# Late modulation vectors on TensorE instead of VectorE, and FFN loads in program order

## The chip, the core and the metric

The kernel runs on one core of one Trainium2 chip. A core has engines that each run their own queue of instructions in order: TensorE (PE in the profile, with its weight loads as PEld), VectorE (DVE), ScalarE (ACT), GpSimd (POOL) and SyncE (SP), which here only starts transfers. Sixteen DMA engines move the data between the large memory (DRAM) and the core's working memory. The metric is the device time of one execution in microseconds (us), the median of several runs. Before the change it is 1277.53 us.

## The reference, cut to what matters

One transformer layer on 2048 rows of 1024 values. Six modulation vectors of 1024 values come from silu(c) times w_mod (1024 x 6144). The first two, sa and ca, shift and scale the first layer norm; ga gates the attention's output; sb and cb shift and scale the second layer norm; gb gates the FFN's output.

```python
def reference(A_x, A_k_cache, A_v_cache, A_wq, A_wo, B_x, B_w_gate, B_w_up, B_w_down, c, w_mod):
    ...
    x = A_x
    mod = (_silu(c) @ w_mod).reshape(c.shape[0], 6, 1, -1)
    sa, ca, ga, sb, cb, gb = (mod[:, 0].copy(), mod[:, 1].copy(), mod[:, 2].copy(), mod[:, 3].copy(), mod[:, 4].copy(), mod[:, 5].copy())
    h = _layernorm(x, axis=-1) * (1 + ca) + sa
    x = x + ga * _A_ref(h, A_k_cache, A_v_cache, A_wq, A_wo)
    h = _layernorm(x, axis=-1) * (1 + cb) + sb
    x = x + gb * _B_ref(h, B_w_gate, B_w_up, B_w_down)
    return x
```

_A_ref is attention: 32 heads of 128, keys and values of four groups cut to their last 512 rows, softmax, and the output projection wo (4096 x 1024). _B_ref is a gated FFN of width 3584: silu(x w_gate) * (x w_up), then w_down.

## The kernel before, in words

All of it lies in fast_path. (A second function, general_path, stands behind a flag for inputs whose scores could grow too large; with these inputs it isn't entered.)

The 2048 rows are cut into four chunks (cc) of 512, the width of one matmul. A first loop runs over 128 steps k, one for each chunk and head: step k computes the scores of head k (emit_s), the queries of head k + 3 (emit_q), then whatever tasks are due at step k (run_tasks), then the weighted sum over the values of head k - 1 (emit_o). A second pair of loops does the FFN: for each chunk seven groups (fg) of four 128-wide slices of the hidden width (emit_gu), then the down projection in two halves (dh) of four row tiles (emit_down). Task numbers go on counting there, from 129.

Tasks are put down by `at(k, f, ...)`: the projection by wo (load_wo, emit_wo, from step 13 on, eight tasks for each quarter of a chunk's heads), the layer norms (plan_ln: statistics, normalised rows, a transposing transfer, and eight affine steps ln_affine with scale and shift), the transposes of attention outputs (xpose_o), the late modulation vectors, and a bound on the scores that sets the flag.

The first two modulation vectors are needed at once and are computed in the opening by mod_cols on TensorE. The other four are late. spread_c writes silu(c) to DRAM and reads it back to all partitions. load_wmT fetches 128 columns of w_mod with a transposing transfer, so that each partition holds one column; mod_dot multiplies this by silu(c) and sums along the row on VectorE, which gives 128 values of the vector as a column (eight such for one vector). cb and sb are used as columns; cb gets 1 added by add_one. The gates ga and gb are needed as rows on all partitions: store_gate turns the columns on VectorE and writes them to DRAM, load_gate reads them back.

The order of instructions is set by a scheduler that works with its own estimates, except where `pin` keeps an instruction in program order. A switch in `stage` says what pin holds: in the first loop transfers and listed VectorE instructions; in the FFN loops neither, since `stage.update(dma=False, steps=False)` stands between the loops. All loads go through SP's one queue by way of fetch (line 664). An instruction on a queue that waits holds up those behind it.

Buffers: PSUM tiles of 512 values come from a set of four (`mm`), for q_ps, a_ps, o_ps and d_ps; pairs of score or gate-and-up tiles from another. Weights of wq, gate and up use seven blocks of set B, with one more block in the storage of v_sb once attention is over (every second FFN group puts a quarter there); wo, down tiles, oq and oT use twelve blocks of set C; hT, the modulated inputs, and pieces of w_mod use four buffers of hpool.

In the FFN loops before the change, a group's gate and up tiles are loaded (load_gu) in the program just ahead of their use, and the first half's down tiles of chunk 0 after its groups:

```python
            if (cc, fg) != (0, 0):
                load_gu(cc, fg)
            if cc > 0:
                load_wd(cc, 0, fg)
```

The scheduler may move them.

Of the kernel before, what the change touches and what calls it, by code (L numbers as in the profile page):

```python
# [9 lines left out]
ALU = mybir.AluOpType  # L10
AX = mybir.AxisListType
BF16 = mybir.dt.bfloat16
FP32 = mybir.dt.float32
# [575 lines left out]
def fast_path(ctx, tc, flag, A_x, A_k_cache, A_v_cache, A_wq, A_wo, B_x, B_w_gate, B_w_up,  # L589
# [3 lines left out]
    nc = tc.nc  # L593
    P = 128
    _, S, D = A_x.shape
    _, Hkv, Sk, Dh = A_k_cache.shape
# [6 lines left out]
    TCW = 512  # L603
    NTC = S // TCW
    QT = TCW // P
    DT = D // P
# [5 lines left out]
    NFG = FT // 4  # L612
# [11 lines left out]
    wm_v = w_mod.rearrange("(dt p) n -> p dt n", p=P)  # L624
# [4 lines left out]
    const = ctx.enter_context(tc.tile_pool(name="const", bufs=1))  # L629
    xpool = ctx.enter_context(tc.tile_pool(name="xres", bufs=1))  # L630
    hpool = ctx.enter_context(tc.tile_pool(name="hT", bufs=4))
# [3 lines left out]
    wk = ctx.enter_context(tc.tile_pool(name="work", bufs=2))  # L635
    sm = ctx.enter_context(tc.tile_pool(name="small", bufs=4))
    psp = ctx.enter_context(tc.tile_pool(name="psum", bufs=4, space=bass.MemoryType.PSUM))
    dp = ctx.enter_context(tc.tile_pool(name="dram", bufs=4, space=bass.MemoryType.DRAM))
# [7 lines left out]
    def blkC(name, shape, dt=BF16):  # L646
        return pc_.tile(shape, dt, name=name, tag="C")

    def mm(name, shape=(P, 512), dt=FP32):
        return psp.tile(list(shape), dt, name=name, tag="mm", bufs=4)  # L650
# [7 lines left out]
    stage = {"dma": True, "steps": False}  # L658

    def pin(ins, what="steps"):  # L660
        return tc.keep_in_program_order(ins) if stage[what] else ins

    def fetch(out, in_):
        pin(nc.sync.dma_start(out=out, in_=in_), "dma")

    def load(out, in_):
        with nc.allow_non_contiguous_dma(reason="weight slice"):
            fetch(out=out, in_=in_)
# [33 lines left out]
    for kv in range(Hkv):  # L702
        pin(nc.sync.dma_start_transpose(
            out=kT[:, kv, :], in_=A_k_cache[0, kv, k0:k0 + W, :]), "dma")
# [10 lines left out]
    ones_bf = const.tile([P, P], BF16, name="ones_bf")  # L715
# [15 lines left out]
    sa, ca1, sb, cb1 = (modT[:, i, :] for i in range(4))  # L731
    ga_bc = const.tile([P, D], FP32, name="ga_bc")
    gb_bc = const.tile([P, D], FP32, name="gb_bc")
# [7 lines left out]
    sil_r = const.tile([DT, P], BF16, name="sil_r")  # L741
# [3 lines left out]
    siluc = const.tile([P, DT], BF16, name="siluc")  # L745
# [12 lines left out]

    c_d = dp.tile([DT, P], BF16, name="c_d", tag="c_d", bufs=1)
    c_bc = const.tile([P, D], BF16, name="c_bc")
    gcol = [const.tile([P, 32], FP32, name=f"gcol{n}") for n in range(2)]
    grow = const.tile([P, 32], FP32, name="grow")
    for n in range(2):
        nc.gpsimd.memset(gcol[n], 0.0)
    wm_cols = {}
    col_d = {}  # L770

    def spread_c():
        fetch(out=c_d, in_=sil_r)
        fetch(out=c_bc.rearrange("p (a b) -> p a b", a=DT), in_=c_d.partition_broadcast(P))

    def load_wmT(vec, j):
        if j % 4 == 0:
            wm_cols[(vec, j // 4)] = hpool.tile([P, 4, D], BF16, name="wmT", tag="hT")
        c0 = vec * D + j * P
        pin(nc.sync.dma_start_transpose(out=wm_cols[(vec, j // 4)][:, j % 4, :],  # L780
                                        in_=w_mod[:, c0:c0 + P]), "dma")

    def mod_dot(vec, j, dst):
        t = wm_cols[(vec, j // 4)]
        junk = wk.tile([P, D], BF16, name="junk", tag="junk", bufs=1)
        pin(nc.vector.scalar_tensor_tensor(out=junk, in0=t[:, j % 4, :], scalar=1.0, in1=c_bc,
                                           op0=ALU.mult, op1=ALU.mult,
                                           accum_out=dst[:, j:j + 1]))

    def add_one(dst):  # L790
        pin(nc.vector.tensor_scalar(out=dst, in0=dst, scalar1=1.0, scalar2=None, op0=ALU.add))

    def store_gate(n):
        d = dp.tile([DT, P], FP32, name="col_d", tag="col_d", bufs=2)
        pin(nc.vector.transpose(out=grow, in_=gcol[n]))
        for q in range(4):
            fetch(out=d[:, 32 * q:32 * q + 32], in_=grow[32 * q:32 * q + DT, :])
        col_d[n] = d

    def load_gate(n, dst):  # L800
        fetch(out=dst.rearrange("p (a b) -> p a b", a=DT), in_=col_d[n].partition_broadcast(P))

    tasks = {}

    def at(k, f, *a):
        tasks.setdefault(k, []).append((f, a))


    hT = {}
# [112 lines left out]
    for t in range(QT):  # L922
        ln_stats(t)
        n = ln_norm(t, t % 2 == 0)
# [5 lines left out]
    for half in range(DH):  # L930
# [6 lines left out]
        for n in range(4 * LEAD):  # L937
            dt, g = (4 * half + n // LEAD, n % LEAD) if half == 0 else (4 + n % 4, n // 4)
            nc.tensor.matmul(q0_ps[g],  # L939
                             lhsT=wq_tiles[(0, 0, dt // 4)][:, dt % 4, g * P:(g + 1) * P],  # L940
                             rhs=hT[("h1", 0)][:, dt, :], start=(dt == 0), stop=(dt == DT - 1))
# [168 lines left out]
            nc.vector.tensor_tensor(out=x1, in0=f, in1=x1, op=ALU.add)  # L1110


    at(0, spread_c)
    for vec, dst, starts in ((2, gcol[0], (1, 9)), (4, cb1, (17, 25)), (3, sb, (33, 41)),
                             (5, gcol[1], (51, 61))):
        for part in range(2):
            for i in range(4):
                at(starts[part] + 2 * i, load_wmT, vec, 4 * part + i)
                at(starts[part] + 2 * i + 3, mod_dot, vec, 4 * part + i, dst)
        k = starts[1] + 10  # L1120
        if vec == 4:
            at(k, add_one, cb1)
        elif vec in (2, 5):
            at(k, store_gate, vec // 5)
            at(k + 3, load_gate, vec // 5, gb_bc if vec == 5 else ga_bc)
    for tt in range(QT, S // P):
        cc, t = divmod(tt, QT)
        at(max((cc - 1) * H - 16, 0) + 2 + 2 * t, load_x, tt)
# [32 lines left out]
    def load_gu(cc, fg):  # L1161

        for nm, v in (("wg", wg_v), ("wu", wu_v)):
            for i in range(2):
                spare = (cc * NFG + fg) % 2 == 1 and nm == "wu" and i == 1
                t = v_blk if spare else blkB(nm, [P, 4, 512])
                load(t, v[:, 4 * i:4 * i + 4, fg * 512:(fg + 1) * 512])
                gu_w[(cc, fg, nm, i)] = t
# [16 lines left out]
    def load_wd(cc, dh, fg):  # L1185
        t = blkC("wd", [P, 4, 512])
        load(t, wd_v[:, 4 * fg:4 * fg + 4, dh * 512:(dh + 1) * 512])
        wd_tiles[(cc, dh, fg)] = t
# [23 lines left out]
    for k in range(NU + 1):  # L1212
# [9 lines left out]
        run_tasks(k)  # L1222
        if k >= 1:
            emit_o(k - 1)
    stage.update(dma=False, steps=False)
    for cc in range(NTC):
        for fg in range(NFG):
            if (cc, fg) != (0, 0):
                load_gu(cc, fg)
            if cc > 0:  # L1230
                load_wd(cc, 0, fg)
            for fi in range(4):
                emit_gu(cc, 4 * fg + fi)
                run_tasks(NU + 1 + (cc * NFG + fg) * 4 + fi)
        for dh in range(DH):
            if dh > 0 or cc == 0:
                for fg in range(NFG):
                    load_wd(cc, dh, fg)
            for t in range(QT):
                last = cc == NTC - 1 and dh == DH - 1 and t == QT - 1  # L1240
                emit_down(cc, dh, t, (256, 128, 128) if last else (512,))
# [41 lines left out]
```

## Time and profile before

| what | value |
|---|---|
| median of 3 runs | 1277.53 us (1277.34 to 1278.34) |
| the profiled execution | 1277.53 us |
| its span, first to last instruction | 1275.8 us |
| mean granted TensorE clock | 0.998 |
| VectorE dot products (L786) | 32, 38.9 us busy |
| transposing loads of w_mod (L780) | 32, on SP |
| DMA, mean over the span | 160 GB/s |

The profile is one execution. Busy times of different engines overlap, so their sum says nothing; what ends the kernel is read from the chain of waits and from the idle time ahead of each engine's instructions. A matmul's record lasts longer than the time after which the next one starts; the pace is read from starts. PEclk gives the granted clock in tenths, by slices of 32 us.

### The profile page before, as it was taken

How to read it: one execution, taken by the hardware profiler on the slowest of the kernel's cores; microseconds unless marked ns; L12 is line 12 of the kernel's file. 1: busy time of each engine (PE TensorE's matmuls, PEld its weight loads, DVE VectorE, ACT ScalarE, POOL GpSimd, SP SyncE). 2: the span in 40 equal slices, each digit the busy share in tenths (PEclk: the TensorE clock that was granted, in tenths of full speed). 3: DMA queues.
4: the chain of work that ended last, by engine and by line, in shares of the span. 5: the costliest groups of instructions: out<-in, count | busy, mean ns of one | idle time of the engine just before them, and what ended most of it. 6: DMA issues, size and time to landing. Idle time of an engine off the chain costs nothing.

```text
span 1275.8 us, 17958 instructions
## 1 busy us (share of the span) xinstructions
PE 1256.8 (99%) x7396; PEld 641.0 (50%) x7537; DVE 606.8 (48%) x1325; ACT 333.7 (26%) x433; POOL 1.3 (0%) x10
## 2 busy tenths in 40 slices
PE   8999999999999999999999999999999999999998
PEld 4555555555555555555554444444444444444444
DVE  4575578966587755576663641221122112221122
ACT  3543333343343433334341111011100111011100
POOL 0000000000000000000000000000000000000000
PEclk9999999999999999999999999999999999999999
DMA  9998556785646563446467474455436454454301
GB/s 269 223 223 197 156 132 187 169 186 154 164 127 173 141 172 118 141 124 141 127 214 231 152 244 137 136 190 172 158 119 211 134 178 151 141 190 136 128 22 48
DMA packets 307868, 204.46 MB, mean 160 GB/s; under 512 B 145601, under 2 KB 305345, under 8 KB 307778
## 3 DMA queue, kind: packets, MB, share of 16 engines
q1 hardware_dynamic: 302866, 199.03, 54.6%
q10 hardware_dynamic: 4912, 4.20, 1.0%
q8 instruction: 61, 1.00, 0.3%
q14 instruction: 29, 0.24, 0.1%
HBM read 165.94 MB, written 4.21 MB: 133 GB/s over the span
## 4 chain that ended last, share of the span: by engine, by line
PE 97%; DVE 1%; issue 1%; ACT 0%; DMA 0%
PE gu_ps L1177 30%; PE a_ps L1095 17%; PE q_ps L1018 17%; PE d_ps L1197 15%; PE o_ps L1063 9%; PE s_ps L1031 8%; PE q_ps L939 1%; DVE junk L954 0%; DVE st L815 0%; DMA x<-in_A_x_dram 0%; PE mod_ps L753 0%; ACT pT L1033 0%; DVE qT L915 0%; ACT xn L831 0%; PE h_ps L926 0%
## 5 line engine op out<-in xcount | busy, mean ns | idle before, releaser
L1033 ACT ACTIVATE pT<-s_ps 128x1024 bf16<-128x1024 f32 x256 | 248.9, 1020 | 357.9 <-PE s_ps L1031 230.5
L1095 PE MATMUL a_ps<-wo,oT 128*128 128x512 bf16 x987 | 240.0, 379 | 1.9
L1018 PE MATMUL q_ps<-hT,wq 128*128 128x512 bf16 x999 | 236.9, 379 | 0.3 <-DVE modT L755 0.3
L1183 DVE TENSOR_TENSOR guT<-gu_ps,sg 128x512 bf16<-128x512 f32 x112 | 77.4, 691 | 283.1 <-ACT sg L1182 283.1
L1177 PE MATMUL gu_ps<-hT,wg 128*128 128x512 bf16 x875 | 209.7, 379 | 1.1
L1182 ACT ACTIVATE sg<-gu_ps 128x512 bf16<-128x512 f32 x112 | 66.9, 597 | 488.7 <-PE gu_ps L1177 431.7
L1197 PE MATMUL d_ps<-wd,guT 128*128 128x512 bf16 (+2 forms) x934 | 193.2, 366 | 0.9
L915 DVE CAST qT<-q_ps 128x512 bf16<-128x512 f32 x128 | 88.2, 690 | 159.7 <-PE q_ps L1018 157.3
L1177 PE MATMUL gu_ps<-hT,wu 128*128 128x512 bf16 x659 | 162.0, 379 | 0.7
L1095 PEld LDWEIGHTS <-oT 128*128 128x128 bf16 x1024 | 100.2, 98 | 120.6
L1018 PEld LDWEIGHTS <-wq 128*128 128x128 bf16 x1000 | 97.8, 98 | 117.7 <-issue 0.3
L1197 PEld LDWEIGHTS <-guT 128*128 128x128 bf16 x952 | 90.9, 98 | 103.0
L1063 PEld LDWEIGHTS <-pT 128*128 128x128 bf16 x2048 | 126.8, 98 | 31.0 <-issue 0.4
L1177 PEld LDWEIGHTS <-wg 128*128 128x128 bf16 x896 | 87.6, 98 | 105.5
L1063 PE MATMUL o_ps<-v_sb,pT 128*128 128x130 bf16 x2048 | 137.3, 220 | 0.1
L1031 PE MATMUL s_ps<-qT,kT 128*128 128x512 bf16 x467 | 129.3, 379 | 2.9 <-ACT pT L1033 0.6
L1177 PEld LDWEIGHTS <-wu 128*128 128x128 bf16 x672 | 65.8, 98 | 79.3
L1050 DVE TENSOR_TENSOR oq<-o_ps,rl 128x256 bf16<-128x256 f32 (+2 forms) x256 | 100.4, 419 | 3.7 <-issue 0.2
L1201 DVE TENSOR_TENSOR f<-d_ps,gb_bc 128x512 f32<-128x512 f32 (+2 forms) x34 | 22.4, 660 | 147.1 <-PE d_ps L1197 147.1
L1031 PEld LDWEIGHTS <-kT 128*128 128x128 bf16 x512 | 44.9, 98 | 31.5 <-issue 1.3
L1103 DVE TENSOR_TENSOR acc<-a_ps,acc 128x512 f32<-128x512 f32 x64 | 44.1, 688 | 32.8 <-PE a_ps L1095 32.6
L1177 PE MATMUL gu_ps<-hT,v_sb 128*128 128x512 bf16 x220 | 56.9, 379 | 0.2
(76 smaller groups left out, 401.4 us busy)
## 6 DMA issues: line engine op xcount, KB each, us to landing
wq<-in_A_wq_dram SPq DMA_DIRECT2D x64, 512.0 KB
wo<-in_A_wo_dram SPq DMA_DIRECT2D x64, 512.0 KB
wg<-in_B_w_gate_dram SPq DMA_DIRECT2D x56, 512.0 KB
wd<-in_B_w_down_dram SPq DMA_DIRECT2D x56, 512.0 KB
wu<-in_B_w_up_dram SPq DMA_DIRECT2D x42, 512.0 KB
v_sb<-in_B_w_up_dram SPq DMA_DIRECT2D x14, 512.0 KB
x<-in_A_x_dram SPq DMA_DIRECT2D x16, 256.0 KB
wm<-in_w_mod_dram SPq DMA_DIRECT2D x4, 1024.0 KB
```

The lines of the kernel that those rows point to most:

```text
L915: nc.vector.tensor_copy(out=t, in_=q_ps)
L1018: nc.tensor.matmul(q_ps, lhsT=wq_tiles[(cc, h // 4, dt // 4)][:, dt % 4, (h % 4) * P:(h % 4 + 1) * P], rhs=hT[("h1", cc)][:, dt, :], start ...
L1031: nc.tensor.matmul(s_ps[:, i, :], lhsT=kT[:, kv, j * P:(j + 1) * P], rhs=qT[g], start=True, stop=True)
L1033: nc.scalar.activation(out=p[:, 2 * jj:2 * jj + 2, :], in_=s_ps, func=ACT.Exp, scale=scale)
L1050: nc.vector.tensor_tensor(out=dst, in0=ps[:, s0:s0 + cnt, 0:Dh], in1=sc, op=ALU.mult)
L1063: nc.tensor.matmul(o_slot["ps"][:, s_, :], lhsT=pT[g][:, j, t * P:(t + 1) * P], rhs=v_sb[:, kv, j, 0:VN], start=(j == 0), stop=(j == WT - 1))
L1095: nc.tensor.matmul(a_ps, lhsT=oT[(cc, 2 * q + i)][:, hh % 4, t * P:(t + 1) * P], rhs=wo_tiles[(cc, q, dh, i)][:, hh % 4, :], start=(hh == ...
L1103: nc.vector.tensor_tensor(out=acc[(cc, t)][:, dsl], in0=a_ps, in1=acc[(cc, t)][:, dsl], op=ALU.add)
L1177: nc.tensor.matmul(ps[:, n, :], lhsT=gu_w[(cc, fg, nm, dt // 4)][:, dt % 4, fi * P:(fi + 1) * P], rhs=hT[("h2", cc)][:, dt, :], start=(dt ...
L1182: nc.scalar.activation(out=g, in_=ps[:, 0, :], func=ACT.Silu)
L1183: nc.vector.tensor_tensor(out=guT[(cc, fg)][:, fi, :], in0=ps[:, 1, :], in1=g, op=ALU.mult)
L1197: nc.tensor.matmul(d_ps, lhsT=guT[(cc, f // 4)][:, f % 4, t * P:(t + 1) * P], rhs=wd_tiles[(cc, dh, f // 4)][:, f % 4, c0:c0 + w], start=( ...
```

## The change

Two things are changed.

The late vectors: load_rows now fetches w_mod as it lies, four 128-row blocks by one vector's 1024 columns (1 MB) in one transfer. sil32 holds silu(c) repeated over 32 columns; it is made in the opening by eight VectorE multiplications. mod_rows multiplies on TensorE: two vectors at a time, as four strips of 512 values, each to its own 32 PSUM partitions, in two parts of 16 matmuls (steps 5 and 13 for ga and cb, 21 and 29 for gb and sb). VectorE copies the first part out and adds it to the second; the four rows go to DRAM (row_d). load_gate reads a gate back to all partitions, load_cols reads cb or sb back as columns, 1024 single values, and for cb adds 1 on VectorE.

The FFN's transfers: pin still holds transfers in program order in the FFN loops. load_gu is called one group ahead. In chunk 0 the first half's down tiles are loaded two at a time in its last four groups.

```diff
--- before.py
+++ after.py
@@ -758,47 +758,48 @@
-    c_d = dp.tile([DT, P], BF16, name="c_d", tag="c_d", bufs=1)
-    c_bc = const.tile([P, D], BF16, name="c_bc")
-    gcol = [const.tile([P, 32], FP32, name=f"gcol{n}") for n in range(2)]
-    grow = const.tile([P, 32], FP32, name="grow")
-    for n in range(2):
-        nc.gpsimd.memset(gcol[n], 0.0)
-    wm_cols = {}
-    col_d = {}
-    def spread_c():
-        fetch(out=c_d, in_=sil_r)
-        fetch(out=c_bc.rearrange("p (a b) -> p a b", a=DT), in_=c_d.partition_broadcast(P))
-    def load_wmT(vec, j):
-        if j % 4 == 0:
-            wm_cols[(vec, j // 4)] = hpool.tile([P, 4, D], BF16, name="wmT", tag="hT")
-        c0 = vec * D + j * P
-        pin(nc.sync.dma_start_transpose(out=wm_cols[(vec, j // 4)][:, j % 4, :],
-                                        in_=w_mod[:, c0:c0 + P]), "dma")
-    def mod_dot(vec, j, dst):
-        t = wm_cols[(vec, j // 4)]
-        junk = wk.tile([P, D], BF16, name="junk", tag="junk", bufs=1)
-        pin(nc.vector.scalar_tensor_tensor(out=junk, in0=t[:, j % 4, :], scalar=1.0, in1=c_bc,
-                                           op0=ALU.mult, op1=ALU.mult,
-                                           accum_out=dst[:, j:j + 1]))
-    def add_one(dst):
-        pin(nc.vector.tensor_scalar(out=dst, in0=dst, scalar1=1.0, scalar2=None, op0=ALU.add))
-    def store_gate(n):
-        d = dp.tile([DT, P], FP32, name="col_d", tag="col_d", bufs=2)
-        pin(nc.vector.transpose(out=grow, in_=gcol[n]))
-        for q in range(4):
-            fetch(out=d[:, 32 * q:32 * q + 32], in_=grow[32 * q:32 * q + DT, :])
-        col_d[n] = d
-    def load_gate(n, dst):
-        fetch(out=dst.rearrange("p (a b) -> p a b", a=DT), in_=col_d[n].partition_broadcast(P))
+    sil32 = const.tile([P, DT, 32], BF16, name="sil32")
+    for dt in range(DT):
+        nc.vector.tensor_scalar(out=sil32[:, dt, :], in0=ones_bf[:, 0:32],
+                                scalar1=siluc[:, dt:dt + 1], scalar2=None, op0=ALU.mult)
+    wm_rows = []
+    row_part = []
+    row_d = {}
+    def load_rows(vec, part):
+        t = hpool.tile([P, 4, D], BF16, name="wmr", tag="hT")
+        load(t, wm_v[:, 4 * part:4 * part + 4, vec * D:(vec + 1) * D])
+        wm_rows.append(t)
+    def mod_rows(n, part):
+        ps = mm("row_ps")
+        tiles = [wm_rows.pop(0) for _ in range(2)]
+        for k in range(4):
+            for i in range(4):
+                nc.tensor.matmul(ps[32 * i:32 * i + 32, :], lhsT=sil32[:, 4 * part + k, :],
+                                 rhs=tiles[i // 2][:, k, (i % 2) * 512:(i % 2 + 1) * 512],
+                                 start=(k == 0), stop=(k == 3))
+        if part == 0:
+            r = blkC("row", [P, TCW], FP32)
+            nc.vector.tensor_copy(out=r, in_=ps)
+            row_part.append(r)
+        else:
+            r = row_part.pop()
+            nc.vector.tensor_tensor(out=r, in0=ps, in1=r, op=ALU.add)
+            d = dp.tile([4, TCW], FP32, name="row_d", tag="row_d", bufs=2)
+            fetch(out=d, in_=r[0:P:32, :])
+            row_d[n] = d
+    def load_gate(n, k, dst):
+        fetch(out=dst.rearrange("p (a b) -> p a b", a=2),
+                          in_=row_d[n][k:k + 2, :].partition_broadcast(P))
+    def load_cols(n, k, dst, add_one):
+        src = row_d[n][k:k + 2, :].rearrange("a (b p) -> p (a b)", p=P)
+        with nc.allow_non_contiguous_dma(reason="1024 values to columns"):
+            fetch(out=dst, in_=src)
+        if add_one:
+            nc.vector.tensor_scalar(out=dst, in0=dst, scalar1=1.0, scalar2=None, op0=ALU.add)
     tasks = {}
@@ -1110,19 +1111,14 @@
             nc.vector.tensor_tensor(out=x1, in0=f, in1=x1, op=ALU.add)
-    at(0, spread_c)
-    for vec, dst, starts in ((2, gcol[0], (1, 9)), (4, cb1, (17, 25)), (3, sb, (33, 41)),
-                             (5, gcol[1], (51, 61))):
+    for n, vecs in enumerate(((2, 4), (5, 3))):
         for part in range(2):
-            for i in range(4):
-                at(starts[part] + 2 * i, load_wmT, vec, 4 * part + i)
-                at(starts[part] + 2 * i + 3, mod_dot, vec, 4 * part + i, dst)
-        k = starts[1] + 10
-        if vec == 4:
-            at(k, add_one, cb1)
-        elif vec in (2, 5):
-            at(k, store_gate, vec // 5)
-            at(k + 3, load_gate, vec // 5, gb_bc if vec == 5 else ga_bc)
+            k = 16 * n + 8 * part
+            at(k, load_rows, vecs[0], part)
+            at(k + 2, load_rows, vecs[1], part)
+            at(k + 5, mod_rows, n, part)
+        at(16 * n + 15, load_gate, n, 0, gb_bc if n else ga_bc)
+        at(16 * n + 16, load_cols, n, 2, sb if n else cb1, n == 0)
     for tt in range(QT, S // P):
         cc, t = divmod(tt, QT)
         at(max((cc - 1) * H - 16, 0) + 2 + 2 * t, load_x, tt)
@@ -1222,18 +1218,23 @@
         run_tasks(k)
         if k >= 1:
             emit_o(k - 1)
-    stage.update(dma=False, steps=False)
+    stage.update(steps=False)
     for cc in range(NTC):
         for fg in range(NFG):
-            if (cc, fg) != (0, 0):
-                load_gu(cc, fg)
+            n = cc * NFG + fg + 1
+            if n < NTC * NFG:
+                load_gu(*divmod(n, NFG))
             if cc > 0:
                 load_wd(cc, 0, fg)
+            elif fg >= NFG - 4:
+                for i in range(2):
+                    if 2 * (fg - NFG + 4) + i < NFG:
+                        load_wd(0, 0, 2 * (fg - NFG + 4) + i)
             for fi in range(4):
                 emit_gu(cc, 4 * fg + fi)
                 run_tasks(NU + 1 + (cc * NFG + fg) * 4 + fi)
         for dh in range(DH):
-            if dh > 0 or cc == 0:
+            if dh > 0:
                 for fg in range(NFG):
                     load_wd(cc, dh, fg)
             for t in range(QT):
```

## The prediction

> **What bounds the kernel now.** I read the page first (busy shares, slices, chain), then the stretches by window, then TensorE's own waits, then the chain in order of time, and last the timeline where the change puts new work.
>
> ```profile
> span 1275.8 us, 17958 instructions
> PE 1256.8 (99%) x7396; PEld 641.0 (50%) x7537; DVE 606.8 (48%) x1325; ACT 333.7 (26%) x433; POOL 1.3 (0%) x10
> PEclk9999999999999999999999999999999999999999
> PE 97%; DVE 1%; issue 1%; ACT 0%; DMA 0%
> ...
> 0.00:20.00 20.00, 14.59 (x167) 8.31 (x170) 9.71 (x29) 7.40 (x14) 1.34 (x10) 1.00 1.02 320
> 100.00:200.00 100.00, 99.16 (x674) 54.62 (x686) 64.50 (x149) 37.37 (x42) 0.00 (x0) 1.00 0.66 172
> 900.00:1000.00 100.00, 99.53 (x456) 45.30 (x463) 21.44 (x31) 8.96 (x15) 0.00 (x0) 1.00 0.50 169
> ...
> PE warm_ps L727 <- POOL warm_w L721: 1.5, 1, 1.5
> PE s_ps L1031 <- ACT pT L1033: 0.6, 2, 0.3
> ...
> 745.32 10.74 PE gu_ps L1177 x49
> 756.11 10.74 PE gu_ps L1177 x49
> ...
> 22.17 4.24 PE L939 MATMUL q_ps<-hT,wq 128*128 128x512 bf16 x12
> ```
>
> TensorE is 99% busy, but that row alone proves nothing, because one record lasts 379 ns and records overlap. The chain pieces prove it: one piece of the FFN starts 10.79 us after the other (756.11 - 745.32) and holds 50 matmuls (49 recorded, one missing), so one 128x512 matmul takes 10.79 / 50 = 0.2158 us, piece after piece. The program has 1024 such matmuls for q, 512 for scores, 1024 for wo, 1792 for gate and up, 896 for down: 5248, of which 24 fall in the opening. 5224 x 0.2158 = 1127.3 us. A head's 16 narrow o matmuls fill what is left of an early step: 3.49 - 12 x 0.2158 = 0.90 us; 128 heads give 115.5 us. Sum 1242.8; from the end of the opening (26.4 us) this reaches 1269.2, and the last matmuls end near 1270.5. So between the opening and the tail TensorE loses about 1.3 us in all. The longest waits in its list belong to the opening, none to the FFN. Nothing outside the first 26 us and the last 5 us can be won; whatever is added to TensorE's queue is paid in full.
>
> **What the Trainium skill says.** "TensorE: Matmul & The Clock Gate", Part 3, "Measured speedup vs the span model": matmuls with 32 stationary columns, each with its output at another 32-partition strip, run side by side; three in columns gave 2.38x, four in rows 3.07x. "TensorEngine Tiling (Array Packing)", "Key Properties": a change of the tiling mode drains TensorE. No record of before has a tile other than 128 columns wide, so the trace neither agrees nor disagrees. "DMA: Bandwidth & Descriptors", "Rules for kernel authors": a transfer with a strided last dimension becomes one descriptor per element; before has no such transfer of 4-byte pieces. The first page, Part 1, has TensorE at half clock after an idle window of some 3.4 us; here the 12 q matmuls at 22.17 us average 0.353 us against 0.216, which agrees in kind.
>
> **The change, part by part.** All times against the profiled execution: 1277.53 us, 1.7 more than its span, and equal to the median.
>
> (1) Removed, on VectorE: 32 dot products (group L786, 38.9 us at 1216 ns, with 32 accumulator reads of 83 ns), two 32x32 transposes, and the 32 transposing loads and eight small stores on SP. VectorE is 48% busy and TensorE waits for it for less than 2 us in all, in the opening. Gain: nothing on the path. Also gone is SP's stop between writing c_d and reading c_bc.
>
> (2) Added, on TensorE: four bursts of 16 matmuls (L779), at steps 5, 13, 21 and 29, 32 columns wide, 512 elements each. One after the other they cost 64 x 0.2158 = 13.8 us. Successive ones go to different column strips, so I take the 3.07x of the skill for four: 4.5 us (estimate). Each burst enters and leaves the narrow mode; a drain I take as what a record lasts beyond the pace, 0.379 - 0.216 = 0.163 us (estimate); eight make 1.3. Sum 5.8 us. Bounds: perfect fourfold overlap and no drain 3.5 us; no overlap 13.8 + 1.3 = 15.1 us. There is no idle TensorE time to hide any of it.
>
> Do the bursts wait for their data? The first needs two 1 MB loads, which SP can issue from about 25 us. Ahead of the second's end lie some 3.5 MB; at the 210 GB/s of the stretch from 40 to 60 us this is 17 us: landed by 42, used at about 45. The others have 5 to 10 us more. Nothing, with 3 us of margin for the first.
>
> (3) Added, eight small multiplications on VectorE in the opening (sil32, about 0.13 us each as a small VectorE row such as siluc's copy shows): 1.0 us before the third tile's statistics. On TensorE the order also changes: the first two mod_ps groups (64 matmuls) now stand ahead of the third and fourth tiles' transposes. Both end before the last w_mod tile arrives (19.90 us, the DMAs at 320 GB/s), which ends last there. Zero, within -1.7 and +1: the matmuls at half clock are worth 4.24 - 12 x 0.2158 = 1.65 us if the clock should now stay up.
>
> (4) Added, a wait on VectorE. Scale cb1 now comes by way of DRAM: row_d is written, then ga_bc and the 8x128 column values are fetched, and L802 adds one. L802 stands, in VectorE's fixed order, just after xn of the seventh tile and ahead of the acc copy of step 15. In before these are:
>
> ```profile
> 84.14 0.69 DVE L915 CAST qT<-q_ps 128x512 bf16<-128x512 f32 x1 [0.32 <-PE q_ps L1018]
> 84.75 0.54 DVE L834 TENSOR_SCALAR xn<-x,mv 128x1024 bf16<-128x1024 bf16 x1
> 85.87 0.69 DVE L1101 COPY acc<-a_ps 128x512 f32<-128x512 f32 x1 [0.58 <-PE a_ps L1095]
> 89.16 1.89 PE L1095 MATMUL a_ps<-wo,oT 128*128 128x512 bf16 x8
> ...
> 24.83 0.38 SPq L664 DMA_DIRECT2D c_d<-sil_r  x1
> 29.91 0.36 SPq L664 DMA_DIRECT2D c_bc<-c_d  x1
> ```
>
> VectorE reaches L802 at 85.3 + 2.9 (two bursts) = 88.2 us. SP: row_d waits for the second burst's sum. That burst ends at about 73.5 + 2.9 = 76.4, the sum at 77.4. Behind it on SP, by before's durations: row_d 0.3, wo 0.6, wq 0.5, four oT transposes 6.0, hT 1.3, wq 0.5, ga_bc 0.7, the column fetch about 0.8: issued at 88.1. Landing: the only small transfer that before waits for, c_d, took from 25.2 to 29.9 = 4.7 us under a full queue. So 92.8. How long can TensorE go on? The psum pool has four buffers: a_ps of step 15, two of o_ps, q_ps of step 16; the fifth request, a_ps of step 16, comes at 89.16 + 2.9 = 92.1. After landing VectorE still has L802, one half of statistics (0.68) and the acc copy (0.69) before a buffer is free: 92.8 + 0.16 + 1.37 + 0.1 = 94.4. TensorE waits 94.4 - 92.1 = 2.3 us; with a little for the 1024 pieces, 2.6 us. Bounds: 0 (landing within 2.3 us) and about 6 (landing after 8). The second set, step 32, is read only by the later affines: nothing.
>
> (5) The FFN's loads. Now every one stays in program order, and a group's four gate and up loads are issued one group ahead. They need buffers that group fg-1 gave back, so each starts at the start of group fg and is needed 13.8 us later (64 x 0.2158). Demand: five loads of 0.52 MB in 13.8 us = 190 GB/s, in the last four groups of the first chunk six, 228 GB/s; the opening ran at 320. Before has loads behind other loads on the same queue and no TensorE wait, so there is nothing to gain; what can be lost is a load stuck behind one whose buffer is not free. The candidates are the last two down tiles of a half (issued some 5 us before the half ends, as the two of before at 1241.07, needed 4.3 us after it starts) with the next chunk's second group behind them, which has 24 + 14 us left; and SP's read of flag, which stands ahead of the third group's loads and is over before group 0 (20.7 us with the wo matmuls) is. Zero.
>
> Sum: 5.8 + 2.6 = 8.4 us: 1277.5 + 8.4 = 1285.9.
>
> **The rivals.** About 0.2%, 2.6 us, can be told from no change.
> - The VectorE wait doesn't reach TensorE (landing in 2 us): 1277.5 + 5.8 = 1283.3. For it: the queue is lighter without transposing loads (stretch 80 to 100 us: DMA share 0.80). Against: SP is late by the row_d wait. 17%.
> - The narrow matmuls don't overlap: 15.1 + 2.6 = 17.7, 1295.2. For it: nothing in the trace shows overlap, and their weights are loaded anew for each. Against: the skill's measurement. 16%.
> - Program order makes FFN loads late, say 3 us in each of the four groups with six loads: 8.4 + 12, 1298. Against: the margins of (5). 5%.
> - Not slower: fourfold overlap without drains (3.5), no VectorE wait, and the opening's q matmuls at full clock (-1.65), because transposes and warm-up matmuls now run nearer to them: +1.9, 1279.4. It decides from 1280.1 down. Against: the idle time before 19.90 us, which lets the clock fall, is set by the loads and stays. 12%.
>
> **How the numbers follow.** The forecast 50% (own range 1282.5 to 1290), the others as given. 1280.5 to 1296 takes in the first three and leaves out the last two. Slower: 50 + 17 + 16 + 5 = 88; of the last 12, 2 faster (the opening gains more) and 10 within.
>
> **What would show it.** Burst records 128*32 spaced by about 70 ns rather than 216; a TensorE wait of 2 to 3 us near 92 us, put down to VectorE or the column fetch; L802's idle time of 4 to 5 us; FFN windows at 99.5 busy again; 26.4 us as the opening's end. Wrong if the chain shows DMA inside the FFN, or if the FFN ends earlier relative to its start than now.

## The result, and the profile after

The changed kernel takes 1283.48 us, the median of 6 runs (1283.05 to 1285.36), against 1277.19 us for the kernel before in runs beside it (1276.31 to 1278.34). The ratio is 1.0052 with a 95% interval of 1.0039 to 1.0065: slower by 6.3 us. The profiled execution took 1283.05 us with a span of 1281.3 us, 5.5 us more than the span before. What follows explains these 5.5 us of the two profiles; the medians lie 0.8 us further apart.

The page of the kernel after, its span, the busy times and the chain by engine:

```profile
span 1281.3 us, 17945 instructions
PE 1262.1 (99%) x7461; PEld 642.4 (50%) x7601; DVE 577.9 (45%) x1271; ACT 333.9 (26%) x433; POOL 1.2 (0%) x8
PE 96%; SPq 2%; DMA 1%; issue 1%; DVE 0%
```

VectorE lost 28.9 us of work, TensorE gained 5.3 us busy, and the span followed TensorE. New in the chain is SPq, the sequencer of SyncE, which before does not appear: in the opening, from 3.9 to 19.7 us, the chain now runs through SyncE's queue. (The kernel with the new FFN order alone, below, shows SPq 2% as well.)

Two stretches of the kernel before that the prediction does not show, and then the stretches of the kernel after (start:end, length, busy time and count of PE, PEld, DVE, ACT and POOL, then clock, DMA share and GB/s):

```profile
20.00:40.00 20.00, 19.02 (x140) 10.08 (x143) 8.13 (x20) 9.20 (x10) 0.00 (x0) 0.91 0.88 215
40.00:100.00 60.00, 59.63 (x437) 34.12 (x443) 40.67 (x99) 30.58 (x38) 0.00 (x0) 1.00 0.89 208
```

```profile
0.00:20.00 20.00, 16.44 (x151) 8.79 (x153) 10.19 (x34) 7.40 (x14) 1.23 (x8) 0.91 0.97 308
20.00:40.00 20.00, 18.13 (x160) 10.05 (x160) 8.63 (x23) 9.21 (x10) 0.00 (x0) 1.00 1.10 309
40.00:100.00 60.00, 58.34 (x444) 32.59 (x450) 33.20 (x85) 28.59 (x36) 0.00 (x0) 1.00 0.83 223
900.00:1000.00 100.00, 99.53 (x456) 45.34 (x464) 21.44 (x31) 8.81 (x16) 0.00 (x0) 1.00 0.44 140
```

The FFN is busy as before, 99.53 of 100 us. Between 40 and 100 us TensorE is busy for 58.34 us, 59.63 before: it lost time there. The stretch with the lower granted clock, 0.91, has moved from 20 to 40 us into the first 20 us. In the first 20 us the loads run at 308 GB/s, 320 before; this looks like nothing, and turns out to be a part of the answer. TensorE's own waits, with the total, how often and the longest:

```profile
PE mod_ps L753 <- DMA wm<-in_w_mod_dram: 1.8, 2, 1.3
...
PE a_ps L1096 <- DVE acc L1102: 1.3, 1, 1.3
```

Neither stood in the list before. The first is in the opening, the second is the VectorE wait of the prediction. The place of the first burst, in the timeline of the kernel before and then of the kernel after (start, length, what):

```profile
43.79 1.89 PE L1018 MATMUL q_ps<-hT,wq 128*128 128x512 bf16 x8
45.52 1.07 PE L1063 MATMUL o_ps<-v_sb,pT 128*128 128x130 bf16 x16
```

```profile
43.78 1.89 PE L1019 MATMUL q_ps<-hT,wq 128*128 128x512 bf16 x8
45.60 1.05 PE L779 MATMUL row_ps<-wmr,sil 128*32 128x512 bf16 x16
46.58 1.08 PE L1064 MATMUL o_ps<-v_sb,pT 128*128 128x130 bf16 x16
```

From the start of the q matmuls to the start of the weighted sums it is 1.73 us before and 2.80 us after, so the burst costs TensorE 1.07 us. Sixteen narrow matmuls take 0.98 us of it, 61 ns each, counted from the first of them to the next wide one. The other 0.09 us lie ahead of them: the first narrow one starts 0.31 us after the wide one before it, where wide ones follow each other at 0.216 us. The place of the VectorE wait, from the timeline of the kernel after:

```profile
86.01 0.43 SPq L664 DMA_DIRECT2D modT<-row_d  x1
...
91.36 0.17 DVE L802 TENSOR_SCALAR modT<-modT 128x8 f32<-128x8 f32 x1 [3.92 <-DMA modT<-row_d]
...
92.05 0.67 DVE L1102 COPY acc<-a_ps 128x512 f32<-128x512 f32 x1
...
92.77 1.89 PE L1096 MATMUL a_ps<-wo,oT 128*128 128x512 bf16 x7 [1.29 <-DVE acc L1102]
```

The fetch of cb1 is issued at 86.01 us, VectorE stands still for 3.92 us until it has landed, and the acc copy behind it frees a psum buffer for which TensorE has then waited 1.29 us.

One place has become shorter. The timeline of the kernel before, and then of the kernel after:

```profile
180.60 0.67 DVE L915 CAST qT<-q_ps 128x512 bf16<-128x512 f32 x1
...
181.32 0.39 PE L1063 MATMUL o_ps<-v_sb,pT 128*128 128x130 bf16 x4
```

```profile
185.46 1.07 PE L1064 MATMUL o_ps<-v_sb,pT 128*128 128x130 bf16 x16
```

Before, the last four of a head's 16 weighted sums start only once VectorE's copy of the queries has ended (180.60 + 0.67 = 181.27), which by the starts costs TensorE 0.31 us. After, with fewer VectorE instructions, this copy starts 0.23 us ahead of the sums (185.23) instead of 0.92 us behind the first of them (179.68), and all 16 run in one piece. This gain stands in every kernel with the new vectors, and in none with the old.

For the experiments one line of each profile does most of the work, that of the weighted sums (o_ps): its first start is the end of the opening, its last start the end of the first loop. Before and after (minimum, median and maximum duration in ns, then first and last start):

```profile
L1063 PE MATMUL o_ps<-v_sb,pT x2048: 218/220/220, 30.7 to 669.3; 128*128 128x130 bf16 x187
```

```profile
L1064 PE MATMUL o_ps<-v_sb,pT x2048: 220/220/230, 30.7 to 674.8; 128*128 128x130 bf16 x187
```

Opening to 30.7 us in both; loop 638.6 and 644.1 us; from there to the last down projection (1270.3 and 1275.8) 601.0 us in both. The whole 5.5 us lies in the loop. Since all 2048 of these matmuls are recorded, the two traces can be laid beside each other step by step. Within the loop the kernel after falls behind at five places, by 1.07 to 1.08 us at each burst (4.33 us in all) and by 1.45 us at the VectorE wait, and it gains the 0.31 us shown above: 4.33 + 1.45 - 0.31 = 5.47 us. At no other step do the two differ by more than 0.03 us.

### The profile page after: what moved, and what is told of

It is laid out like the page before. It is cut to its first block, busy times and chain, and to the rows that moved or that the text cites. A ratio compares the mean times of both kernels' runs of the same rounds, so it can differ in the third digit from the quotient of the medians.

```text
span 1281.3 us, 17945 instructions
## 1 busy us (share of the span) xinstructions
PE 1262.1 (99%) x7461; PEld 642.4 (50%) x7601; DVE 577.9 (45%) x1271; ACT 333.9 (26%) x433; POOL 1.2 (0%) x8
## 4 chain that ended last, share of the span: by engine, by line
PE 96%; SPq 2%; DMA 1%; issue 1%; DVE 0%
PE gu_ps L1173 30%; PE a_ps L1096 17%; PE q_ps L1019 16%; PE d_ps L1193 15%; PE o_ps L1064 9%; PE s_ps L1032 8%; SPq L664 1%; SPq L703 1%; DMA modT<-row_d 0%; DMA wq<-in_A_wq_dram 0%; PE row_ps L779 0%; DVE st L816 0%; SPq L848 0%; DVE qT L916 0%; DVE acc L1102 0%
## 5 line engine op out<-in xcount | busy, mean ns | idle before, releaser
L1179 DVE TENSOR_TENSOR guT<-gu_ps,sg 128x512 bf16<-128x512 f32 x112 | 77.4, 691 | 284.1 <-ACT sg L1178 284.1
```

The lines of the kernel that those rows point to most:

```text
L1179: nc.vector.tensor_tensor(out=guT[(cc, fg)][:, fi, :], in0=ps[:, 1, :], in1=g, op=ALU.mult)
```

## The experiments

Twelve kernels, each timed beside the kernel before on the same chip (4 to 22 executions each; the kernel before had medians from 1277.19 to 1277.46 us). They were timed in three groups and on two chips, so a difference of two medians of the table is less certain than a ratio. The last three columns come from the profiled execution of each: first o_ps, first to last o_ps, last o_ps to last d_ps.

| kernel | median, us | ratio to before (95%) | opening to | loop | FFN |
|---|---|---|---|---|---|
| before | 1277.4 | 1 | 30.7 | 638.6 | 601.0 |
| after | 1283.48 | 1.0052 (1.0039 to 1.0065) | 30.7 | 644.1 | 601.0 |
| vectors only | 1285.12 | 1.0065 (1.0051 to 1.0079) | 30.1 | 644.1 | 602.0 |
| FFN only | 1276.53 | 0.9995 (0.9987 to 1.0003) | 29.5 | 638.6 | 601.0 |
| late addition | 1281.38 | 1.0037 (1.0024 to 1.0051) | 30.4 | 642.6 | 601.1 |
| strip by strip | 1283.55 | 1.0053 (1.0039 to 1.0067) | 30.5 | 644.3 | 601.0 |
| bursts twice | 1287.20 | 1.0079 (1.0065 to 1.0093) | 30.9 | 648.7 | 601.0 |
| one strip | 1293.11 | 1.0124 (1.0108 to 1.0139) | 30.7 | 654.5 | 601.0 |
| long pieces | 1283.26 | 1.0050 (1.0036 to 1.0063) | 30.9 | 643.6 | 601.1 |
| late addition, old FFN | 1284.25 | 1.0053 (1.0039 to 1.0066) | 30.7 | 642.7 | 601.7 |
| aligned | 1281.79 | 1.0034 (1.0021 to 1.0048) | 29.5 | 644.1 | 601.0 |
| before, shifted | 1278.95 | 1.0013 (1.0007 to 1.0020) | 31.1 | 638.6 | 601.0 |
| vectors only, aligned | 1282.70 | 1.0041 (1.0029 to 1.0053) | 29.3 | 643.4 | 601.3 |
| late addition, aligned | 1280.33 | 1.0022 (1.0014 to 1.0031) | 29.3 | 642.7 | 601.0 |

### Vectors only, FFN only

The change cut in two: the new vectors with the FFN loops of before, and the reverse.

```diff
-    stage.update(steps=False)
+    stage.update(dma=False, steps=False)
...
-            n = cc * NFG + fg + 1
-            if n < NTC * NFG:
-                load_gu(*divmod(n, NFG))
+            if (cc, fg) != (0, 0):
+                load_gu(cc, fg)
...
-            if dh > 0:
+            if dh > 0 or cc == 0:
```

> The new vectors with the FFN loops as they were before. Theory: the whole difference comes from the vectors (four bursts of 1.08 us, one VectorE wait of 1.4 us), so this is 5.5 to 6.5 us slower than before, as the changed kernel is, and its FFN lasts as long. Rival: part of the 6.3 us comes from the FFN's loads; then this is less than 4.5 us slower, or, if the new order of loads had gained something that the vectors ate up, more than 7.5 us slower.

> The VectorE dot products of before with the changed FFN loops. Theory: no TensorE wait in the FFN either way, so within 0.5 us of before. Rival: one load ahead and program order cost or gain 1 us or more, seen as a DMA wait of TensorE between 780 and 1270 us or as a shift of the FFN's first to last down projection.

The FFN's new order alone changes nothing that can be measured (0.9995, and the interval takes in 1), though its median is 0.9 us below before, more than the 0.5 us expected. Its profile is 1.2 us shorter, all of it in the opening (29.5 against 30.7), where nothing was edited: its 12 q matmuls at 21.67 us took 2.80 us against the 4.24 us of the profile before, at a clock of 1.00 where before has 0.91. So an opening that is not edited can differ by 1.2 us from one execution to another. The vectors alone cost 7.7 us, past the 5.5 to 6.5 expected and past the 7.5 us of the rival in which the new order of loads gains something. The runs of the two kernels overlap, though (1283.52 to 1285.67 us, and 1283.05 to 1285.36 for the whole change), so what the new order gains is read from the profiles alone. The timeline of the vectors-only kernel shows a wait that neither before nor after has:

```profile
748.81 0.55 DVE L835 TENSOR_SCALAR xn<-x,mvl 128x1024 bf16<-128x1024 bf16 x1 [3.42 <-DMA hT<-xn]
...
752.62 1.38 DVE L856 TENSOR_SCALAR hT<-hT,modT 128x512 bf16<-128x512 bf16 x4 [2.67 <-DMA hT<-xn]
...
754.66 1.89 PE L1173 MATMUL gu_ps<-hT,wg 128*128 128x512 bf16 x8 [0.76 <-DVE guT L1179]
```

VectorE waits for transposes of the last layer norm, the group's product stands behind it, and TensorE misses a buffer. In the old FFN order these transposes are queued behind four down tiles; in the new one they come later, and no TensorE work waits for them. The same instructions in the kernel before finish in time: there VectorE's affine steps begin 0.60 us after the group's first gate matmuls (745.92 - 745.32), here 2.34 us after them (752.62 - 750.28). So something in the vectors half had made these transfers slower.

### Late addition

```diff
+    def add_one(dst):
+        pin(nc.vector.tensor_scalar(out=dst, in0=dst, scalar1=1.0, scalar2=None, op0=ALU.add))
...
-        at(16 * n + 16, load_cols, n, 2, sb if n else cb1, n == 0)
+        at(16 * n + 16, load_cols, n, 2, sb if n else cb1, False)
+    at(30, add_one, cb1)
```

> The changed kernel, with the addition of 1 to cb1 put at step 30 instead of right behind its fetch at step 16. Theory: VectorE no longer stands still for 3.92 us near 91 us, TensorE's wait of 1.3 us for acc at step 16 is gone, and the time falls by 1.3 to 1.5 us against the changed kernel: 4.2 to 5.0 us slower than before. Rival: TensorE would have waited there anyway (psum buffers, the weights of wo), or the stall is made good later; then still 5.5 to 6.5 us slower.

The loop shrank by 1.5 us and the wait for acc is gone from the list. The stretch of this kernel from 40 to 100 us has 1.24 us more of busy TensorE than in the kernel after:

```profile
40.00:100.00 60.00, 59.58 (x459) 33.65 (x466) 34.41 (x84) 28.74 (x37) 0.00 (x0) 1.00 0.83 227
```

The median fell by 2.1 us, to 3.9 us above before; by the ratio it is 0.37% or 4.7 us, within the 4.2 to 5.0 expected. What is left in the loop, 642.6 - 638.6 = 4.0 us, is the four bursts, 4.33 us, less the 0.31 us gained near 181 us.

### Strip by strip, bursts twice, one strip

```diff
-        for k in range(4):
-            for i in range(4):
+        for i in range(4):
+            for k in range(4):
```

> The changed kernel with the loops of mod_rows exchanged: the same 16 matmuls per burst, but the four to one column strip stand together. Theory: the fourfold overlap needs successive matmuls on different strips; then a burst takes up to 16 x 0.216 = 3.45 us instead of 0.98, and the four add up to 9.9 us: 12 to 16.5 us slower than before. Rival: TensorE overlaps them in any order, or the pace of a 32-column matmul is simply a quarter of a 128-column one; then unchanged, 5.5 to 6.5 us slower than before.

The rival was right. In the program as built the four matmuls of a strip do stand together, so the scheduler has not undone the edit. The burst, from this kernel's timeline:

```profile
45.42 1.08 PE L779 MATMUL row_ps<-wmr,sil 128*32 128x512 bf16 x16
46.43 1.08 PE L1064 MATMUL o_ps<-v_sb,pT 128*128 128x130 bf16 x16
```

1.01 us between the starts, as with alternating strips. If matmuls started strictly in order, only the three changes of strip could overlap, and a burst would need 13 x 0.2158 = 2.8 us. But this run alone cannot tell overlap from a matmul that is short because it is narrow. Two more do. Bursts twice issues the block of 16 two times over; one strip sends all 16 to the first 32 columns, with the loops exchanged as above:

```diff
-                nc.tensor.matmul(ps[32 * i:32 * i + 32, :], lhsT=sil32[:, 4 * part + k, :],
+                nc.tensor.matmul(ps[0:32, :], lhsT=sil32[:, 4 * part + k, :],
```

> The changed kernel with the 16 matmuls of each burst issued twice over (the second pass starts the sums again, so the result is the same). Theory: within a burst a narrow matmul takes a quarter of 0.2158 us, 0.054, and a burst has a further fixed 0.2 us for entering and leaving the narrow mode; then each burst grows by 16 x 0.054 = 0.86 us and the whole by 3.5 us, to 8.5 to 10 us slower than before. Rival: there is no fixed part, a narrow matmul costs 1.02 / 16 = 0.064 us; then 4.1 us more, and a burst of 32 takes 2.1 us. Second rival: the bursts' time is mostly a fixed price of the mode, then 1 us more or less.

> The changed kernel with all 16 matmuls of a burst sent to the first 32 columns, one sum after the other; the four rows that are stored are then four copies of the last quarter, so the late gates, shift and scale are other values, while every instruction and transfer keeps its place (the two VectorE steps read 32 partitions instead of 128). Theory: the fourfold pace comes from four strips working at the same time, which TensorE arranges although the same strip is named four times in a row when the loops are exchanged; on a single strip nothing is left to overlap, a burst takes 16 x 0.2158 = 3.45 us, and the whole is 12 to 16.5 us slower than before. Rival: a matmul of 32 columns and 512 elements takes a quarter of the time by itself; then unchanged, 5 to 6.5 us slower than before.

Timeline of bursts twice, then of one strip:

```profile
45.80 1.91 PE L780 MATMUL row_ps<-wmr,sil 128*32 128x512 bf16 x32
47.64 1.08 PE L1065 MATMUL o_ps<-v_sb,pT 128*128 128x130 bf16 x16
```

```profile
45.63 3.63 PE L779 MATMUL row_ps<-wmr,sil 128*32 128x512 bf16 x16
49.19 1.08 PE L1064 MATMUL o_ps<-v_sb,pT 128*128 128x130 bf16 x16
```

On one strip 16 matmuls take 49.19 - 45.63 = 3.56 us, 0.11 more than 16 x 0.2158 = 3.45: a narrow matmul is no shorter than a wide one. On four strips 32 take 1.84 us and 16 take 0.98, so 16 more cost 0.86 = 16 x 0.0538, a quarter each. A burst of 16 costs TensorE 1.08 us in all, the 0.09 us ahead of its first matmul counted, so some 0.22 us are the fixed price of entering and leaving the narrow mode. The theory held in both, and its 0.2 us for that price was right. The records of the single matmuls in the traces say the same: with alternating strips four matmuls start within 10 ns and the next four 0.22 us later; strip by strip, too, four start within 40 ns, and the next four 0.22 us later; on one strip each starts 0.22 us after the one before. Strip by strip the program's first four matmuls belong to one strip, so those that start together are not the ones that stand together. Bursts twice grew by 4.6 us in the loop, 1.2 more than 4 x 0.86, since the longer burst also made the VectorE wait longer (2.5 us in its list).

### Long pieces

```diff
-        src = row_d[n][k:k + 2, :].rearrange("a (b p) -> p (a b)", p=P)
+        src = row_d[n][k:k + 2, :].rearrange("a (p b) -> (a p) b", b=DT)
```

> The changed kernel with the columns of cb and sb fetched in 128 pieces of 32 bytes instead of 1024 of 4 bytes; the values then stand in another order, so the second layer norm is scaled and shifted by permuted vectors. Theory: the pieces are the smaller part of the 5.3 us that this fetch takes, [...] then it lands after 4 to 5 us, and TensorE's wait of 1.3 us for acc falls to between 0 and 1: 4.5 to 6 us slower than before. Rival: the 1024 pieces make the time; then it lands within 3 us, TensorE does not wait at all, and the time is that of the kernel with the late addition, 0.31% above before. Second rival: the size of the pieces does not matter, 5.3 us again and 1.3 us of waiting.

TensorE's wait in this kernel:

```profile
PE a_ps L1096 <- DVE acc L1102: 0.8, 1, 0.8
```

With an eighth of the pieces the fetch of cb1 still takes 4.9 us of 5.3, and TensorE waits 0.8 us instead of 1.3. So the 1024 single elements, of which the prediction had thought, are not what makes the fetch long. Whether they cost the 0.4 us is not shown: with all 1024 pieces the same fetch took from 4.7 us (vectors only, aligned, where TensorE waited 0.6 us) to 6.5 us (bursts twice), so a single profile of 4.9 us lies within what the runs vary by, and the second rival, that the size of the pieces does not matter, stands. What the rest of the time is, the queue or the way to DRAM and back, no run separates. The medians, 1283.26 and 1283.48, don't tell the two apart.

### Late addition with the old FFN

The late addition, with the FFN loops of the vectors-only kernel.

> The late addition of 1 together with the FFN loops as they were before. Theory: the wait of 0.76 us that TensorE had near 754 us with the new vectors and the old FFN order (VectorE's affine steps of the last layer norm stood ahead of the group's product and waited for transposes behind four down tiles) is a matter of that order and comes back: the profile shows it again and the time is 0.8 us above the late addition with the new FFN order, so 0.37 to 0.5% above before. Rival: it was a chance of that one execution; then no such wait, and 0.25 to 0.4% above before.

The wait came back, 0.56 us, and the FFN took 601.7 us: it is no chance. The time, 0.53% above before, is just past the 0.5% expected. The median is 2.9 us above that of the late addition, more than the profiled execution shows (1.0, of which 0.6 in the FFN and 0.3 in the opening). Its five runs fall into two groups, two at 1282.30 and 1282.37 us and three from 1284.25 to 1284.70, and the profiled one is of the first; what the others lose no profile shows.

### Where the tiles begin

Why should transfers be slower with the new vectors? The rate of the loads gives a hint, here over the first 30 us in 40 slices, before and after.

```profile
GB/s 0 0 63 314 385 298 284 247 300 377 365 382 388 385 388 385 384 385 389 384 385 389 381 374 378 363 183 35 232 267 168 190 242 162 202 328 385 320 136 14
```

```profile
GB/s 0 0 128 333 284 221 315 370 362 351 386 363 352 347 345 350 347 347 348 348 348 350 359 336 345 350 328 217 52 140 253 207 212 224 234 224 284 345 369 340
```

At full load mostly 384 to 389 GB/s before, 345 to 350 after, at a time when both issue the same loads of x, w_mod and wq. What differs is where they land. The change removes c_bc (2048 bytes in each partition), two gcol and grow (3 x 128) and adds sil32 (512): everything allocated behind moves by 1920 bytes. In the programs as built the x tiles began at byte 34816 = 68 x 512, and now begin at 32896 = 64 x 512 + 128; hT, w_mod and all weight tiles move alike. The test is an unused block, of 1920 bytes in the changed kernel, of 128 bytes in the kernel before.

```diff
     sil32 = const.tile([P, DT, 32], BF16, name="sil32")
+    pad = const.tile([P, 960], BF16, name="pad")
```

```diff
     grow = const.tile([P, 32], FP32, name="grow")
+    pad = const.tile([P, 64], BF16, name="pad")
```

> The changed kernel with an unused block of 1920 bytes behind sil32, so that the tiles after it (x, hT and w_mod, the weights) begin again at multiples of 512 bytes within a partition, as they did before the change; with the change they begin 128 bytes further. Theory: the start of the tiles sets the rate of the loads; at full load the FFN's loads run again at 376 to 385 GB/s instead of 343 to 358, the first 20 us at 320 instead of 308, TensorE's wait of 1.3 us for w_mod near 12 us goes or shrinks, and the time falls by 0 to 1 us against the changed kernel (which is TensorE bound after the opening). Rival: the rate goes with the new vectors' transfers or with the program's size and stays at 350.

> The kernel before with an unused block of 128 bytes behind grow: the same instructions, every tile after it 128 bytes further. Theory: full-load rate 343 to 358 GB/s instead of 376 to 385, first 20 us at 308 instead of 320, and 0.5 to 3 us slower than before, from the opening and from a wait for the last layer norm's transposes near 750 us. Rival: the start of the tiles makes no difference: 376 to 385 GB/s, within 0.3 us of before.

The same row of the aligned kernel, then of the shifted kernel before:

```profile
GB/s 0 0 107 311 328 183 280 348 348 366 380 384 384 388 388 381 385 389 385 385 388 389 367 381 383 343 189 204 272 184 191 242 174 254 318 380 336 300 385 399
```

```profile
GB/s 0 0 101 330 322 180 313 324 350 381 381 370 352 350 348 350 350 345 348 350 344 348 358 344 347 352 340 262 111 273 217 174 204 264 141 273 380 377 254 28
```

The rate goes with where the tiles begin: 380 to 389 again in the aligned kernel, 344 to 350 in the shifted one, whose instructions are those of before. All fourteen profiles fall in line, the five with tiles at multiples of 512 bytes mostly above 380 at full load, the nine others near 350. In time: aligned 1.7 us below the changed kernel, more than the 0 to 1 us expected, and no run of the one overlaps those of the other (1281.72 to 1282.39, 1283.05 to 1285.36); shifted 1.5 us above before (1.0013, interval above 1). In the aligned kernel the opening ends at 29.5 us; in all eight profiles with the new vectors and shifted tiles it ends between 30.1 and 30.9. The expected wait near 750 us did not show in the profile of before, shifted; that execution was among its faster ones (1277.92 of a median of 1278.95), and where the rest of its 1.5 us goes stays open.

The Trainium skill has a cause of this kind: "DMA: Bandwidth & Descriptors", "How a descriptor splits into AXI transactions", says that a piece is cut into transactions of 256 bytes, and that one which does not start at a multiple of 256 bytes fetches bytes that it does not use. By that count a weight row of 1024 bytes that begins 128 bytes further would go from four transactions to five (an estimate from that page). But the page speaks of reading, and here it is the place written to that moved. The measured loss is 9% (385 to 350); the transactions themselves no run here shows, so this cause stays open.

> The new vectors with the FFN loops of before, tiles at multiples of 512 bytes again. Theory: TensorE's wait of 0.76 us (0.56 in the other run) for guT near 754 us came from the slower loads ahead of the last layer norm's transposes; it goes, and the time is 1 to 2.5 us below that of the new vectors with the old FFN loops, 0.4 to 0.55% above before. Rival: the wait belongs to the order of the loads and stays at 0.5 us or more: 0.6% or more above before.

> The changed kernel with both repairs, the late addition of 1 and the tiles at multiples of 512 bytes. Theory: only the four bursts are left, 4.0 to 4.3 us in all: 0.25 to 0.36% above before. If the faster loads shorten the opening beyond that of before, down to 0.2% above. Rival: the alignment gives nothing in time, then as the late addition alone, 0.37% above.

With aligned tiles the vectors-only kernel loses most of its FFN wait. From its timeline:

```profile
750.50 1.89 PE L1174 MATMUL gu_ps<-hT,wu 128*128 128x512 bf16 x8
752.51 1.89 PE L1174 MATMUL gu_ps<-hT,wg 128*128 128x512 bf16 x8
```

These eight start 2.01 us after the others, where 8 x 0.2158 = 1.73 would do: 0.28 us late, against 0.93 (754.66 - 752.00 - 1.73) with shifted tiles. So 0.65 of the 0.93 us go with the slow loads. The rest does not belong to the old order alone, for the kernel before has that order and no wait: even with aligned tiles SyncE takes 6.46 us over the four transposes, 6.71 with shifted ones and 5.29 in the kernel before. What else in the new vectors slows them stays open. In the aligned kernel the wait for acc near 91 us is shorter too, 0.6 us, which makes its loop 0.7 us shorter (643.4); the changed kernel with aligned tiles still has 1.3 us there, so this is not the alignment alone. The late addition with aligned tiles comes to 1280.33 us, 2.9 above before (0.22%, at the lower end of what was expected); in the profile 4.1 more in the loop and 1.4 less in the opening. No version with the new vectors beats the kernel before, as their bursts have no idle TensorE time to go to.

## Why the prediction was right, and where it was not

Right: the side, the bound by TensorE, and the two costs it named. The forecast was 1285.9, 2.4 above the measured 1283.48, within its own range. The number alone would have pointed elsewhere: the first rival, a VectorE wait that does not reach TensorE, stood at 1283.3. The traces decide. The wait did reach TensorE, and both costs were there, each smaller than forecast.

Step 1, the removed dot products, 0: 0.31 us were gained, at the one place near 181 us where TensorE had waited for VectorE. That the missing dot products are what brings VectorE forward there was not tested by itself.

Step 2, the bursts, 5.8 us: they cost 4.33. Both terms were too large. The overlap is fourfold, not 3.07 (3.45 us, not 4.5), and entering and leaving the narrow mode costs some 0.22 us for a burst, not 2 x 0.163 (0.9 us in all, not 1.3). That the bursts would not wait for their data was right: all four begin 0.31 us after the matmul before them.

Step 3, the opening, 0: right by luck, as a sum of two parts that were not seen. The dip of the clock lies in the first 20 us in all eleven profiles with the new vectors (clock 0.91 there and 1.00 from 20 to 40 us); in the profile before it was the other way round. In the first 20 us TensorE waits for loads anyway, and the 12 q matmuls then run at full clock: 2.80 us instead of 4.24, a gain of 1.44. The working had named this possibility, with 1.65 us (it compared a record with a pace), and argued against it. The aligned kernels end their opening 1.2 to 1.4 us earlier than the profile before. But the FFN-only kernel does so as well, with the opening of before and a clock of 1.00 in both stretches, so this is a gain over executions in which the dip fell late, and that the new order of w_mod groups and transposes is what moves it was not tested by itself. The slower loads took the same amount back (30.1 to 30.9 us with shifted tiles, 29.3 to 29.5 with aligned ones). The eight multiplications for sil32 took 0.216 us each, not 0.13.

Step 4, the VectorE wait, 2.6 us: the chain was right link by link, the sizes were not. SyncE issued the fetch at 86.0 us, not 88.1, because the sum was ready earlier (row_d issued at 76.50, not 77.4) and the four oT transposes took 5.21 us, not 6.0; the fetch took 5.3 us, not 4.7. The wait was 1.3 us in TensorE's list and cost 1.45 us at that step.

Step 5, the FFN, 0: right on top of the old vectors (0.9995). With the new ones the FFN's order keeps the last layer norm out of the way and saves 0.6 to 1.0 us of the FFN in the profiled executions, 1.6 and 2.9 us by the medians of the two pairs (the second pair ran on two chips); the difference between these is not explained.

Missing altogether: that a change of small constants moves every tile behind them, and with it the rate of all loads. Aligned against changed, this is worth 1.7 us. The sum of what was found is 4.33 (bursts) + 1.45 (wait) - 0.31 (VectorE's relief) = 5.47 us in the loop and nothing in the opening, where an earlier dip and slower loads cancel: the 5.5 us between the two spans.

## What to carry to other kernels

When a kernel is bound by one engine, moving work to it costs its full time even where it packs perfectly: four narrow matmuls side by side took a quarter of the time each, and every burst of them 0.22 us more. A consumer of a value that goes by way of DRAM should not stand in an engine's fixed order right behind the fetch: here 14 steps of delay cost nothing and removed the wait. Before the sizes of costs are added up, lay the two traces beside each other step by step: the loop's total alone hides a gain of 0.31 us behind the bursts. After any edit of buffers compare the load rate of the two profiles at full load, and where it differs, where the tiles begin.

## What the runs showed of the hardware that was not expected

Loads whose tiles begin 128 bytes past a multiple of 512 ran at 345 to 350 GB/s at full load, at the multiple at 384 to 389, with the same instructions; other offsets were not measured. Matmuls on different 32-column strips overlap fourfold even when the program names one strip four times in a row (1.01 us for 16, 3.56 us on a single strip). The Trainium skill, "TensorE: Matmul & The Clock Gate", Part 3, "The mechanism", has weight loads pulled ahead in a window but matmuls strictly in order, and with the latter this measurement does not agree.
